# A constant tile for the warm-up, V's first block earlier, the gate's transpose by DMA, and a last tile split at 384

## The chip, the cores and the metric

The kernel runs on one core of one Trainium2 chip. A core has five engines with a queue of instructions each: TensorE (PE in the profile, with its weight loads as PEld), VectorE (DVE), ScalarE (ACT), GpSimd (POOL) and SyncE (SP), which here only issues transfers. They meet through semaphores. The metric is the device time of one execution in microseconds (us). Four runs of the kernel before gave 165.85, 166.08, 166.55 and 167.09 us, median 166.31.

## The reference, cut to what matters

One input x (2048 tokens, 512 wide) goes through two mixers, and a gate for each token mixes their outputs:

```python
g = _sigmoid((x * gate_w).sum(-1, keepdims=True))
# A: attention over 8 keys of the past, 2 tokens apart, 32 heads of 16
qkv = x @ wqkv
logits = einsum("bhsd,bhswd->bhsw", q, kg) * Dh ** -0.5     # kg: k at s - 2 * w, masked below 0
a = einsum("bhsw,bhswd->bhsd", softmax(logits), vg) @ wo    # heads joined again
# B: an MLP over the tokens
h = _layernorm(x)
u = gelu(einsum("bsd,sf->bdf", h, w1) + b1)                 # 1792 hidden rows
b = transpose(einsum("bdf,fs->bds", u, w2) + b2)
out = g * a + (1 - g) * b
```

All inputs are bfloat16.

## The kernel before, in words

The work comes in stages, and PE runs through them in a fixed order: warm-up matmuls on a tile of ones; transposes of the first 512 tokens of x on PE with fillers between them, and the first q projection (L571, L562, L590); the other projections (L649); the MLP's first product (L859, 14 hidden tiles of 16 matmuls); its second product (L886, 16 output tiles of 128 tokens) with the attention's output projection added into the same PSUM bank (L895).

The program is a list of operations with what each reads and writes. A planner inside the kernel (`_Sched`) gives each a modelled duration, runs a list schedule, and so writes out the order of every engine and its waits; `prio` pushes an operation ahead (negative) or back. PE's operations made by `PE(...)` are chained and stay in the order of the text; those added with `A("pe", ...)` - the score sums (`f_sum`) and the gate's transpose (`f_te`) - go where the planner puts them.

Loads. SP's queue issues, in the order of the text: x tiles 0 and 2, half of wq, wk, then for blocks 1 to 3 of 512 tokens x itself (`ld_x`) and a transposed copy by DMA (`ld_xt`, called xT1 to xT3), wv, then w1's seven blocks (1 MB each, `w1_0` to `w1_6`, in five slots of SBUF that are used again) with wo among them, and w2's eight blocks. w1_1 onward is held until a VectorE-side sum by DMA (`qd0_1`) is done; w1_3 waits for the score sums of the first half of the tokens, because its slot is xT's. ScalarE's queue issues x tiles 1 and 3 and the other half of wq. POOL's queue issues gate_w, b1 and b2 at the start, and later accumulating transfers and the broadcast of attention weights.

The bias rows and gate_w are turned into columns by three small PE transposes (`f_tb`, L662 to L664) and copied out by VectorE (L669 to L671).

Attention. VectorE multiplies q with shifted k for all heads, adds the four sub-blocks, and PE sums over each head's dimensions (`f_sum`, L718, and with it for the first half the gate's dot product, L713). Softmax runs on ScalarE and VectorE. VectorE then multiplies the weights with shifted V and adds, one tile of 256 tokens after another (8 tiles); L895 reads each.

The gate. ScalarE clips the dot product and takes an exp (`zexp`) into `EB`, laid out along tokens in the free dimension, the same value in 32 partitions. `f_te` turns it with four 128x128 PE transposes into PSUM bank 3, and VectorE makes 1 + exp, its reciprocal (`OMG`, the weight of the MLP) and `C2`, OMG times the second bias (L803 to L806). The output evictions (L906 and, for the last tile, L932 and L935) scale by OMG and add C2. The last output tile is made in two halves of 256 columns, in two PSUM banks, evicted by ScalarE and VectorE and stored from two queues.

PSUM banks of the projections go round a ring of seven (`ring`), then of three for V.

Of the kernel before, what the change touches and what calls it, by code (L numbers as in the profile page):

```python
# [280 lines left out]
class _Mem:  # L281
# [17 lines left out]
    def view(self, name, dtype, dims, extra=0, p0=0, np_=128):  # L299
        base = self.arena[:].bitcast(dtype)  # L300
        pst = base.ap[0][0]
        esz = mybir.dt.size(dtype)
        o = self.off[name]
        assert o % esz == 0
        return bass.AP(base.tensor, p0 * pst + o // esz + extra, [[pst, np_]] + [list(d) for d in dims])


def bass_gated_mix__sliding_local_dilated__mixer_token_mlp__prompt_kernel(nc, A_x, A_wqkv, A_wo, B_x, B_w1, B_b1, B_w2, B_b2, gate_w, out, dbg=None):
    with contextlib.ExitStack() as es:
# [19 lines left out]
        m.region("RB", UT_ * 2)  # L329
        m.region("E32", D * 4)  # L330
        m.region("EB", D * 2)
        m.region("IDENT", 128 * 2)
        m.region("ONES", 128 * 2)
        m.region("OUTS", 5 * D * 2)
# [59 lines left out]
        RB = view("RB", BF16, [(1, UT_)])  # L394
        E32 = view("E32", FP32, [(1, D)])
        EB = view("EB", BF16, [(1, D)])
        OUTS = view("OUTS", BF16, [(D, 5), (1, D)])
        IDENT = view("IDENT", BF16, [(1, 128)])
        ONES = view("ONES", BF16, [(1, 128)])
        ONES4 = view("ONES", BF16, [(0, 4), (1, 128)])  # L400
        RP = view("RP", BF16, [(1, 32)])
        GWREP = view("GWREP", BF16, [(32, 4), (1, 32)])
        MASK = view("MASK", BF16, [(PAD, NW), (1, PAD)], np_=32)
# [36 lines left out]
        def sub(ap_, offs, dims):  # L440
            return bass.AP(ap_.tensor, ap_.offset + offs, [list(ap_.ap[0])] + [list(d) for d in dims])
# [8 lines left out]
        def act(o_, i_, f_, **kw):  # L450
# [3 lines left out]
        GELU = "gelu_apprx_tanh_and_others"  # L454


        A("pool", lambda e: e.memset(ONES, 1.0), 0.25, writes=["ones"], name="ones")
        A("pool", lambda e: e.affine_select(out=IDENT, in_=ONES, pattern=[[1, 128]], compare_op=ALU.is_equal,
                                            fill=0.0, base=0, channel_multiplier=-1),
          0.4, reads=["ones"], writes=["ident"], name="ident")  # L460
        A("pool", lambda e: e.memset(sub(KH[0], 0, [(KR, 4), (1, PAD)]), 0.0), 0.2, writes=["kpad"], name="kpad")
        A("pool", lambda e: e.memset(sub(V5, 0, [(VR, 4), (1, PAD)]), 0.0), 0.2, writes=["vpad"], name="vpad")

# [20 lines left out]
        def load(name, dst, src, nbytes, writes, transpose=False, queue="sp", issue=0.5, order=True, deps=(), after=()):  # L484
            ds = sch.dsem(name)

            def fn(e):
                if transpose:
                    return e.dma_start_transpose(dst, src)
                return e.dma_start(dst, src)  # L490
            op = sch.dma(queue, fn, nbytes, ds, issue=issue, writes=writes, deps=list(deps) + late_dep[0],
                         after=list(after) + ([last_ld[queue]] if order and queue in last_ld else []), name=name)
            if order:
                last_ld[queue] = op
            return op
# [4 lines left out]
        def ld_w(name, tn, d0, d1, res):  # L500
            load(name, WQKV[:, d0:d1, tn * D:(tn + 1) * D], wqkv_v[:, d0:d1, tn * D:(tn + 1) * D], (d1 - d0) * 128 * D * 2, [res])

        def ld_xt(sb):
            load("xT%d" % sb, XT[:, :, sb * 512:(sb + 1) * 512], x2d[sb * 512:(sb + 1) * 512, :], int(1.4 * 512 * D * 2), ["xt%d" % sb],
                 transpose=True, issue=3.3)
# [14 lines left out]
        xq(2, "sp")  # L520
        xq(3, "act")
        load("wk", WQKV[:, 0:4, D:2 * D], wqkv_v[:, 0:4, D:2 * D], 4 * 128 * D * 2, ["wk"], deps=[x1ld])
        for k_ in range(1, 4):
            ld_x(4 * k_, 4)
            ld_xt(k_)
        load("gw", GWR, gate_w.rearrange("(t p) -> t p", p=128), 1024, ["gwr"], issue=1.0, queue="pool")
        load("b1", B1R, B_b1.rearrange("(t p) -> t p", p=128), 4096, ["b1r"], issue=1.0, queue="pool")
        load("b2", B2R, B_b2.rearrange("(t p) -> t p", p=128), 4096, ["b2r"], issue=1.0, queue="pool")
        ld_w("wv", 2, 0, 4, "wv")

        def ld_w1(j):
            w1ld[j] = load("w1_%d" % j, W1H[j], w1v[:, :, 256 * j:256 * j + 256], S * 256 * 2, [W1R[j]] + (XTALL if j in (3, 4) else []), order=j < 3,
# [5 lines left out]

        ld_w1(0)

        def f_warm(n):
            def fn(e):
                ins = None
                for _ in range(n):
                    ins = e.matmul(ps[:, 7, :], lhsT=ONES, rhs=ONES4, start=True, stop=True)
                return ins
            return fn

        chain = [None]

        def PE(fn, dur, reads, writes, name, prio=0):
            op = A("pe", fn, dur, reads=reads, writes=writes, after=([chain[0]] if chain[0] is not None else []), name=name, prio=prio)
            chain[0] = op
            return op

        PE(f_warm(5), 2.1, ["ones"], ["b7"], "warm")

        def f_fill(n):
            def fn(e):
                ins = None  # L560
                for _ in range(n):
                    ins = e.matmul(ps[:, 0, 0:256], lhsT=ONES, rhs=sub(ONES, 0, [(0, 2), (1, 128)]), start=True, stop=True)  # L562
                return ins
            return fn

# [33 lines left out]
        def pe_q0(hb, dt):  # L599
            PE(f_q0(hb, dt), 0.44, ["xt0_%d_%d" % (2 * hb + t_, dt // 2) for t_ in range(2)] + ["wq%d" % (dt // 2)], ["b%d" % dl for dl in range(4)],  # L600
               "q0_%d_%d" % (hb, dt))

        pe_tx(0)
        PE(f_fill(1), 0.2, [], ["b0"], "fill0")
        pe_tx(1)
        PE(f_fill(2), 0.4, [], ["b0"], "fill1")
        pe_q0(0, 0)
# [2 lines left out]
        pe_tx(2)  # L610
        pe_tx(3)
        pe_q0(0, 3)
        for dt in range(4):
            pe_q0(1, dt)
        XT0 = ["xt0_%d_%d" % (t, k_) for t in range(4) for k_ in range(2)]
# [42 lines left out]
            PE(f_proj(tn, dl, sb, bank), 0.87, xt_res(sb) + WR[tn], ["b%d" % bank], "pj%s%d_%d" % ("qkv"[tn], dl, sb))  # L658
            evac(tn, dl, sb, bank)

        def f_tb(e):
            e.transpose(out=psb(3)[:, 0:NFT], in_=B1R, identity=IDENT[0:NFT, 0:NFT])  # L662
            e.transpose(out=psb(3)[:, 64:68], in_=GWR, identity=IDENT[0:4, 0:4])
            return e.transpose(out=psb(3)[:, 32:32 + NST], in_=B2R, identity=IDENT[0:NST, 0:NST])  # L664

        for dl in range(4):
            proj(1, dl, 0)
        PE(f_tb, 0.3, ["b1r", "b2r", "gwr", "ident"], ["b3"], "t_b12")
        A("dve", lambda e: e.tensor_copy(out=GWREP, in_=sub(psb(3), 64, [(1, 4), (0, 32)])), 0.2, reads=["b3"], writes=["gwrep"], name="gwrep", prio=-20)  # L669
        A("dve", lambda e: e.tensor_copy(out=B1C, in_=psb(3)[:, 0:NFT]), 0.15, reads=["b3"], writes=["b1c"], name="b1c", prio=-20)  # L670
        A("dve", lambda e: e.tensor_copy(out=B2C, in_=psb(3)[:, 32:32 + NST]), 0.15, reads=["b3"], writes=["b2c"], name="b2c", prio=-20)  # L671
        for dl in range(4):
            proj(0, dl, 1)
            proj(1, dl, 1)
        A("act", act(sub(KH[1], 0, [(KR, 4), (1, PAD)]), sub(KH[0], HS, [(KR, 4), (1, PAD)]), AF.Copy), 0.25,
          reads=["k%d_1" % dl for dl in range(4)], writes=["khalo"], name="khalo")
        for dl in range(4):
# [2 lines left out]
                    proj(tn, dl, sb)  # L680
        ring[0], ring[1] = 0, [0, 1, 2]
        for dl in range(4):
            for sb in range(4):
                proj(2, dl, sb)


# [107 lines left out]
        ld_w1(3)  # L794
        ld_w1(4)

        def f_te(e):
            ins = None
            for k_ in range(4):
                ins = e.transpose(out=psb(3)[:, 128 * k_:128 * k_ + 128], in_=EB[:, 128 * k_:128 * k_ + 128], identity=IDENT)  # L800
            return ins
        A("pe", f_te, 0.5, reads=["eb", "ident"], writes=["b3"], name="t_e", prio=-50, delay=0.5)
        A("dve", lambda e: e.tensor_scalar(out=E1, in0=sub(psb(3), 0, [(256, 2), (32, 4), (128, 2)]), scalar1=1.0, scalar2=None, op0=ALU.add), 0.2,  # L803
          reads=["b3"], writes=["e1"], name="e1", prio=-20)
        A("dve", lambda e: e.reciprocal(out=OMG, in_=E1), 0.2, reads=["e1"], writes=["omg"], name="omg", prio=-20)
        A("dve", tt(C2, OMG, B2C, ALU.mult), 0.12, reads=["omg", "b2c"], writes=["c2"], name="c2", prio=-20)  # L806

# [110 lines left out]
            if half == 1 and i >= LAG:  # L918
                finish_tile(i - LAG)
        lastb = [bank_(), bank_()]  # L920
        CH = ((0, 256), (256, 512))
        for hf, (c0, c1) in enumerate(CH):
            for half in range(2):
                PE(f_ph3(L, lastb[hf], half, c0, c1), 0.77, ["ut%d" % ft for ft in range(7 * half, 7 * half + 7)] + ["w2_%d" % (L // 2)], ["b%d" % lastb[hf]],
# [3 lines left out]
        for hf, (c0, c1) in enumerate(CH):  # L928
            bank = lastb[hf]
            PE(f_wo(L, bank, c0, c1), 0.44, ["ot%d" % (L // 2), "wo"], ["b%d" % bank], "wo%d_%d" % (L, hf))  # L930
            if hf == 0:
                A("act", act(OUTS[:, 4, c0:c1], ps[:, bank, 0:256], AF.Identity, scale=col(OMG, L), bias=col(C2, L)), 0.55,  # L932
                  reads=["b%d" % bank, "omg", "c2"], writes=["outs4"], name="ev%da" % L)
            else:
                A("dve", (lambda bank_, a_, b_: lambda e: e.tensor_scalar(out=OUTS[:, 4, a_:b_], in0=ps[:, bank_, 0:256], scalar1=col(OMG, L),  # L935
                                                                          scalar2=col(C2, L), op0=ALU.mult, op1=ALU.add))(bank, c0, c1), 0.35,
                  reads=["b%d" % bank, "omg", "c2"], writes=["outs4h"], name="ev%db" % L)
            sch.dma("act" if hf == 0 else "sp", (lambda a_, b_: lambda e: e.dma_start(outv[:, L, a_:b_], OUTS[:, 4, a_:b_]))(c0, c1), 65536,
                    ds_out[4] if hf == 0 else ds_last, issue=0.5, reads=["outs4" if hf == 0 else "outs4h"], name="d_out%d_%d" % (L, hf))
# [80 lines left out]
```

## Time and profile before

| | us |
|---|---|
| median of four runs | 166.31 |
| profiled execution, its own time | 165.85 |
| its span | 164.1 |
| PE busy | 159.2 |
| VectorE busy | 150.8 |
| ScalarE busy | 75.3 |
| PE on L859 / L886 / L649 / L895, busy | 48.7 / 49.8 / 38.0 / 15.4 |
| ScalarE's table loads (L955), 11 | 14.1 |

The profile records one execution. "Busy" is the time in which an engine had an instruction in work; matmuls overlap, so their busy time is longer than their share of the chain. Times within the execution count from the start of the span. A line number is that of the kernel before unless the text says otherwise; many vector operations have the line of a helper (L448 for a two-input vector operation, L451 for an activation, L490 and L489 for a load and a transposing load). The chain of waits is followed backward from the last instruction to whatever released it.

### The profile page before, as it was taken

Reading aid. Unit: us, or ns where it says so; the run is one execution under the profiler, and the core shown is the slowest. Engines: PE = TensorE matmul, PEld = TensorE weight load, DVE = VectorE, ACT = ScalarE, POOL = GpSimd, SP = SyncE. Lnnn points to the kernel's source line nnn. Section 1 sums busy time; section 2 is a strip of 40 time slices with the busy share of each in tenths; the row PEclk is TensorE's granted clock in tenths of the full one; section 3 lists DMA queues with packets and bytes.
Section 4 is the critical chain, followed back from the end, with each engine's and each line's share of the span. In section 5 each row is a group of like instructions: output and inputs, shape, how many; then the busy total and the mean of one; then the engine's idle time right before and its main releaser. Section 6 shows DMA issues by size and latency. Waiting matters only on the chain.

```text
span 164.1 us, 2003 instructions
## 1 busy us (share of the span) xinstructions
PE 159.2 (97%) x801; PEld 78.4 (48%) x817; DVE 150.8 (92%) x126; ACT 75.3 (46%) x104; POOL 13.7 (8%) x38
## 2 busy tenths in 40 slices
PE   6999999999999999999999999999999999999993
PEld 2864555555544444444444344444444444444742
DVE  0499999999999999999999999999999999999941
ACT  3366676766682699852211669210121111111164
POOL 7000002020000000005000000005001222000000
PEclk9999999999999999999999999999999999999999
DMA  5999998719498369999999864994995899980013
GB/s 155 298 236 259 221 308 177 144 32 192 116 305 253 94 166 282 289 292 178 166 225 302 253 193 137 292 242 129 274 234 165 170 209 182 211 189 35 32 60 131
DMA packets 44120, 32.11 MB, mean 196 GB/s; under 512 B 7248, under 2 KB 41680, under 8 KB 44112
## 3 DMA queue, kind: packets, MB, share of 16 engines
q1 hardware_dynamic: 40800, 21.96, 50.2%
q0 software_dynamic: 2608, 9.45, 29.3%
q10 hardware_dynamic: 704, 0.59, 1.1%
q8 instruction: 6, 0.10, 0.3%
q14 instruction: 2, 0.02, 0.0%
HBM read 18.88 MB, written 2.10 MB: 128 GB/s over the span
## 4 chain that ended last, share of the span: by engine, by line
PE 95%; DMA 2%; issue 1%; DVE 1%
PE ps L859 29%; PE ps L886 29%; PE ps L649 23%; PE ps L895 8%; PE ps L590 2%; DMA arena<-in_A_x_dram 2%; PE ps L718 1%; PE ps L571 1%; PE ps L713 1%; DVE arena L935 0%; DVE arena L583 0%; PE ps L800 0%; PE ps L562 0%; PE ps L662 0%; PE ps L664 0%
## 5 line engine op out<-in xcount | busy, mean ns | idle before, releaser
L448 DVE TENSOR_TENSOR arena<-arena 128x4096 bf16<-128x4096 bf16 (+8 forms) x79 | 131.8, 1719 | 1.0
L886 PE MATMUL ps<-arena 128*128 128x512 bf16 (+1 forms) x234 | 49.8, 366 | 0.2
L859 PE MATMUL ps<-arena 128*128 128x512 bf16 x218 | 48.7, 379 | 0.3
L451 ACT ACTIVATE arena<-ps,arena 128x512 bf16<-128x512 f32 (+1 forms) x30 | 21.8, 729 | 58.7 <-PE ps L895 37.7
L451 ACT ACTIVATE arena<-ps 128x512 bf16<-128x512 f32 (+3 forms) x53 | 32.9, 629 | 18.7 <-PE ps L649 11.1
L649 PE MATMUL ps<-arena 128*128 128x512 bf16 x172 | 38.0, 379 | 0.2
L886 PEld LDWEIGHTS ps<-arena 128*128 128x128 bf16 x238 | 23.3, 98 | 25.3
L859 PEld LDWEIGHTS ps<-arena 128*128 128x128 bf16 x224 | 21.7, 98 | 26.6 <-ACT arena L451 0.4
L649 PEld LDWEIGHTS ps<-arena 128*128 128x128 bf16 x176 | 19.8, 113 | 17.7 <-issue 0.2
L895 PE MATMUL ps<-arena 128*128 128x512 bf16 (+1 forms) x66 | 15.4, 366 | 0.1
L955 ACT ACT_TABLE_LOAD x11 | 14.1, 1283 | 2.5 <-issue 2.3
L786 POOL DMA_DIRECT2D arena<-arena x8 | 4.3, 561 | 73.9 <-DVE arena L448 73.9
L895 PEld LDWEIGHTS ps<-arena 128*128 128x128 bf16 x68 | 6.7, 98 | 7.2
L688 DVE BATCH_NORM_STATS2 arena<-arena 128x6 f32<-128x512 bf16 x16 | 9.9, 679 | 0.2 <-DMA arena<-in_A_x_dram 0.2
L451 ACT ACTIVATE arena<-arena 128x16 f32<-128x16 f32 (+5 forms) x10 | 6.8, 679 | 6.7 <-DVE arena L448 6.6
L702 DVE TENSOR_SCALAR arena<-arena 128x512 bf16<-128x512 bf16 x16 | 5.5, 418 | 0.0
L583 DVE COPY arena<-ps 128x256 bf16<-128x256 bf16 x4 | 1.1, 292 | 4.6 <-PE ps L571 4.6
L828 POOL DMA_DIRECT2D arena<-arena x3 | 3.6, 1200 | 19.0 <-DVE arena L448 19.0
L743 POOL DMA_DIRECT2D arena<-arena x2 | 2.5, 1234 | 29.2 <-DVE arena L699 20.5
L590 PE MATMUL ps<-arena 128*128 128x256 bf16 x32 | 4.0, 274 | 0.2 <-DVE arena L583 0.2
L935 DVE TENSOR_SCALAR arena<-ps,arena 128x256 bf16<-128x256 f32 x1 | 0.5, 545 | 3.7 <-PE ps L895 3.7
L590 PEld LDWEIGHTS ps<-arena 128*128 128x128 bf16 x32 | 3.3, 114 | 0.7 <-DVE arena L583 0.7
(39 smaller groups left out, 20.1 us busy)
## 6 DMA issues: line engine op xcount, KB each, us to landing
arena<-in_B_w_dram SPq DMA_DIRECT2D x7, 1024.0 KB, 7.2
arena<-in_B_w_dram SPq DMA_DIRECT2D x8, 896.0 KB, 8.5
arena<-arena POOLq DMA_DIRECT2D x5, 1024.0 KB, 7.9
arena<-arena POOLq DMA_DIRECT2D x8, 512.0 KB, 11.0
out_dram<-arena SPq DMA_DIRECT2D x15, 128.0 KB, 1.7
arena<-in_A_x_dram SPq DMA_DIRECT2D x3, 512.0 KB, 4.9
arena<-in_A_wqkv_dram SPq DMA_DIRECT2D x2, 512.0 KB, 4.5
arena<-in_A_wo_dram SPq DMA_DIRECT2D x1, 512.0 KB, 9.6
```

Source lines behind the costliest of these rows:

```text
L448: return lambda e: e.tensor_tensor(out=o_, in0=a_, in1=b_, op=op_)
L451: return lambda e: e.activation(out=o_, in_=i_, func=f_, **kw)
L590: ins = e.matmul(ps[:, dl, hb * 256:hb * 256 + 256], lhsT=sub(WQKV, dt * 3 * D + dl, [(4, 128)]), rhs=XT[:, dt, hb * 256:hb * 256 + 256], ...
L649: ins = e.matmul(ps[:, bank, :], lhsT=sub(WQKV, dt * 3 * D + tn * D + dl, [(4, 128)]), rhs=XT[:, dt, sb * 512:(sb + 1) * 512], start=(dt = ...
L688: A("dve", (lambda t_: lambda e: e.bn_stats(out=ST6[:, t_, :], in_=X[:, t_, :]))(t), 0.67, reads=["x%d" % t], writes=["st%d" % t], name="s ...
L702: A("dve", (lambda t_: lambda e: e.tensor_scalar(out=X[:, t_, :], in0=X[:, t_, :], scalar1=col(RSTD, t_), scalar2=col(NMR, t_), op0=ALU.mu ...
L786: prev = sch.dma("pool", (lambda d_, s_: lambda e: e.dma_start(d_, s_))(dst, src), 524288, sch.dsem("av%d_%d" % (h, c)), issue=1.0, reads= ...
L828: sch.dma("pool", (lambda o_, i_: lambda e: e.dma_start(o_, i_, accum_op=ALU.add, max_dma_last_dim=4096))(pw(0, 4), pw(4, 4)), 1800000, sc ...
L859: ins = e.matmul(ps[:, bank, :], lhsT=W1H[ft // 2][:, st, 128 * (ft % 2):128 * (ft % 2) + 128], rhs=X[:, st, :], start=(st == 0), stop=(st ...
L886: ins = e.matmul(ps[:, bank, 0:c1 - c0], lhsT=W2S[i // 2][:, ft, 128 * (i % 2):128 * (i % 2) + 128], rhs=UT[:, ft, c0:c1], start=(ft == 0) ...
L895: ins = e.matmul(ps[:, bank, 0:c1 - c0], lhsT=OT[:, i // 2, dl, 128 * (i % 2):128 * (i % 2) + 128], rhs=WO[:, dl, c0:c1], start=False, sto ...
L955: e.preload_act_table_set(want)
```

## The change

It has these parts.

- The warm-up matmuls and the fillers read a constant that the program framework writes before the kernel's body, and not the kernel's own tile of ones. The warm-up is five matmuls of 512 columns and four of 128, and it waits for nothing. The filler between the first two transposes of x is dropped.
- The bias and gate_w transposes move from behind the first K projections to the middle of the first q projection, into another PSUM bank.
- On SP's queue wv goes ahead of xT3, and xT3 ahead of the last block of x. On PE the V projection of the first 512 tokens goes ahead of the q and k projections of the second half of the tokens.
- The gate's exp is turned by one transposing DMA from SBUF to SBUF on SP's queue; VectorE reads the result from SBUF. PE's four transposes go.
- The last output tile is split at column 384.

The planner makes a new order from this. What the changed program's order shows beside the moved operations: the first half's score sums come after 32 matmuls of the MLP's first product instead of 24, the second half's after 200 instead of 192; VectorE runs two more q-k products ahead of the statistics of x tiles 12 to 15; the gate's addition comes after the first half's softmax sums instead of before them; the transposing DMA stands on SP between w1_4 and w1_5; ScalarE loads tables 7 times instead of 11.

```diff
-        A("pool", lambda e: e.memset(ONES, 1.0), 0.25, writes=["ones"], name="ones")
+        A("pool", lambda e: e.memset(ONES, 1.0), 0.25, writes=["ones"], name="ones", prio=-90)
...
-        for k_ in range(1, 4):
+        for k_ in range(1, 3):
             ld_x(4 * k_, 4)
             ld_xt(k_)
+        ld_w("wv", 2, 0, 4, "wv")
+        ld_xt(3)
+        ld_x(12, 4)
         load("gw", GWR, ...
         load("b1", B1R, ...
         load("b2", B2R, ...
-        ld_w("wv", 2, 0, 4, "wv")
...
-        def f_warm(n):
-            def fn(e):
-                ins = None
-                for _ in range(n):
-                    ins = e.matmul(ps[:, 7, :], lhsT=ONES, rhs=ONES4, start=True, stop=True)
-                return ins
-            return fn
+        C1 = nc.const_aps.tensor(1.0, (128, 128), BF16)
+
+        def f_warm(e):
+            ins = None
+            for n_ in (512,) * 5 + (128,) * 4:
+                ins = e.matmul(ps[:, 7, 0:n_], lhsT=C1, rhs=nc.const_aps.tensor(1.0, (128, n_), BF16), start=True, stop=True)
+            return ins
...
-        PE(f_warm(5), 2.1, ["ones"], ["b7"], "warm")
+        PE(f_warm, 2.6, [], ["b7"], "warm")
...
-                    ins = e.matmul(ps[:, 0, 0:256], lhsT=ONES, rhs=sub(ONES, 0, [(0, 2), (1, 128)]), start=True, stop=True)
+                    ins = e.matmul(ps[:, 0, 0:256], lhsT=C1, rhs=nc.const_aps.tensor(1.0, (128, 256), BF16), start=True, stop=True)
...
         pe_tx(0)
-        PE(f_fill(1), 0.2, [], ["b0"], "fill0")
         pe_tx(1)
         PE(f_fill(2), 0.4, [], ["b0"], "fill1")
...
         pe_q0(0, 3)
+        PE(f_tb, 0.17, ["b1r", "b2r", "gwr", "ident"], ["b4"], "t_b12")
+        # with its three VectorE copies, now out of bank 4
         for dt in range(4):
             pe_q0(1, dt)
...
         for dl in range(4):
             proj(1, dl, 0)
-        PE(f_tb, 0.3, ["b1r", "b2r", "gwr", "ident"], ["b3"], "t_b12")
-        # with its three VectorE copies, out of bank 3
         for dl in range(4):
             proj(0, dl, 1)
             proj(1, dl, 1)
+        for dl in range(4):
+            proj(2, dl, 0)
...
         for dl in range(4):
-            for sb in range(4):
+            for sb in range(1, 4):
                 proj(2, dl, sb)
...
-        A("pe", f_te, 0.5, reads=["eb", "ident"], writes=["b3"], name="t_e", prio=-50, delay=0.5)
-        A("dve", lambda e: e.tensor_scalar(out=E1, in0=sub(psb(3), 0, [(256, 2), (32, 4), (128, 2)]), scalar1=1.0, scalar2=None, op0=ALU.add), 0.2,
-          reads=["b3"], writes=["e1"], name="e1", prio=-20)
+        sch.dma("sp", lambda e: e.dma_start_transpose(EBT, EB), 400000, sch.dsem("ebt"), issue=0.6, reads=["eb"], writes=["ebt"], name="ebt", prio=-50)
+        A("dve", lambda e: e.tensor_scalar(out=E1, in0=sub(EBT, 0, [(256, 2), (32, 4), (128, 2)]), scalar1=1.0, scalar2=None, op0=ALU.add), 0.2,
+          reads=["ebt"], writes=["e1"], name="e1", prio=-20)
...
-        CH = ((0, 256), (256, 512))
+        CH = ((0, 384), (384, 512))
```

## The prediction

> **What bounds the kernel now.** I read the busy shares first, then TensorE's waits, then the chain that ended last, then the timeline at the places that the diff touches.
>
> ```profile
> span 164.1 us, 2003 instructions
> PE 159.2 (97%) x801; PEld 78.4 (48%) x817; DVE 150.8 (92%) x126; ACT 75.3 (46%) x104; POOL 13.7 (8%) x38
> ```
>
> TensorE (PE) is busy for 97% of the span, VectorE (DVE) for 92%. So there are two candidates, and the waits decide between them.
>
> ```profile
> PE ps L545 <- POOL arena L457: 1.1, 1, 1.1
> PE ps L590 <- DVE arena L583: 0.2, 1, 0.2
> PE ps L571 <- DMA arena<-in_A_x_dram: 0.2, 1, 0.2
> ```
>
> These are all of PE's waits (total, times, longest): 1.5 us, all before 5.2 us. After that PE never waits, for V's load, the gate or VectorE's sums. The chain of waits shows the same, with the pieces that the diff touches:
>
> ```profile
> 0.82 2.60 DMA arena<-in_A_x_dram
> ...
> 3.55 0.58 PE ps L571 x4
> 4.13 0.21 PE ps L562
> 4.35 0.40 PE ps L571 x4
> 4.75 0.02 issue
> 4.77 0.30 DVE arena L583
> 5.07 0.05 issue
> 5.12 1.50 PE ps L590 x12
> ...
> 12.84 0.11 PE ps L662
> ...
> 61.69 0.22 PE ps L800 x4
> ...
> 161.48 0.03 issue
> 161.50 0.55 DVE arena L935
> ```
>
> Columns: start, length, what. The start hangs on the landing of x tile 0 (3.42), not on the warm-up matmuls. L562 is the first filler, L662 begins the bias transposes (0.16 with L663 and L664), L800 is the transpose that goes. What PE does not execute any more, or executes inside one of its few holes, is gain, microsecond for microsecond; what is moved elsewhere is worth nothing unless PE starts to wait.
>
> **Part by part.** Sums are against the profiled execution: span 164.1, its time 165.85, so 1.7 lies around the span. It is the fastest of the four runs; the median, 166.31, is 0.46 above it. I add the change to the median.
>
> *Warm-up without the memset.* PE is let go at about 0.8 (the first loads start at 0.82) but waits until 1.07 for the ones (L457). The constant is there by 0.5, so the warm-up begins about 0.26 earlier. Its five 512-column matmuls start 0.427 apart and 128-column ones 0.107 apart at this clock: 5 x 0.427 + 4 x 0.107 = 2.56, ending at 3.37, before x lands at 3.42. The transposes start at 3.55 as before: no gain of itself. The clock is the unknown. Starts of matmuls in the trace tell when it is granted: 128 columns take 0.107 until 4.57, 256 columns take 0.110 from then on. So full clock comes 3.50 after the first matmul, and in this execution almost nothing but transposes ran before it. An earlier warm-up can save nothing here, and at most 0.26 where the release is late. I take 0 and keep 0.26. The Trainium skill ("TensorE: Matmul & The Clock Gate", What's actually happening) says that the gate looks at a free-running window of about 3.4 us, so that the release varies with where the first matmul falls; 3.50 agrees. By it the release would move by less than 0.26, or by a whole window; the sum stays as it is.
>
> *First filler gone (L562, 0.21).* Behind it are x tile 1's transposes, VectorE's copy (0.30) and the first projection at 5.12. Without it that would be 4.91. But the projection needs wq's first half, issued at 1.27 and landing 3.6 later, 4.9; x tile 0 took 0.13 from landing to matmul, so 5.0. Gain 0.12, between 0 and 0.21.
>
> *Bias transposes moved ahead of the second half of q (L662 to L664, 0.16).* Their new place is where PE stands idle for 0.11 (the matmul at 7.34 ends its slot, the next starts at 7.45, waiting for VectorE's copy). Of 0.16 taken out at 12.84, 0.05 comes back: gain 0.11. Their three POOL loads were issued from 1.48 to 2.72, landing 3.9 to 4.3 later, by 6.65, before 7.2. They use bank 4, so the first K projection now waits for the three copies on VectorE; these end about 8.2, the projection is at 9.4. The copies (0.35) go partly into VectorE's hole of 0.24 before L625.
>
> *V block 0 moved up; its weights' load ahead of xT3 and x12.* The matmuls are the same, 0.863 a projection. The projections of xT1 began at 12.94, now at 12.7, so V starts at 12.7 + 8 x 0.863 = 19.6. Its load takes the queue place of x12 (issued 13.86, landed 4.9 later, 18.8): 0.8 of cover. If that cover goes, PE waits. x12 takes the place of wv on SP (issued 18.58, landed 4.1 later, 22.7); xT3 keeps its place, and the first W1 load after them too. VectorE runs two products (2.2 each) ahead of these four statistics, so it comes to them at 13.96 - 0.3 + 2.2 + 2.4 (statistics of x8) + 4.4 = 22.7 and waits about 0.1, where before it waited 0.18. The activations behind them (L697) sit on ScalarE behind eight evictions and run at 27.2, after their input at 25.8. Normalised x is ready at 22.8 + 2.5 + 0.6 + 2.2 + 0.2 + 5.4 = 33.7, its first matmul at 47. Gain 0.
>
> *Gate transpose by DMA.* L800 leaves PE: gain 0.22, whole, as it stood in an unbroken run of matmuls. New wait: the transpose is on SP behind W1's fifth block, and W1's sixth and seventh and all of w2 are behind it. Times: the changed order puts the score sums 8 matmuls later, at 54.3, done 56.2. ScalarE then does the logits (1.88), the clip, one gelu (its matmuls end at 59.7), a table load (1.28) and the exp (0.63): 62.3. On SP, W1's fourth block waits for the score sums (56.2) and lands 5.7 later, 61.9; the fifth is issued then and lands 5.7 to 7.2 later, 67.6 to 69.1. The transpose, issued at 62.35, comes behind its packets. Price of one: no row has SBUF to SBUF. The nearest is xT3, 512 KB, which landed 1.74 after the load ahead of it (issued 14.49 and landing 6.0 later, 20.5; x12 at 18.8). This one is a quarter: 0.44 to 1.74, so 68.0 to 70.8. VectorE asks for it after L777's addition, which ended at 71.39; without the three small gate operations ahead of it (0.58) and with about 0.4 of holes closed, at 70.4. So VectorE waits 0 to 0.4. Behind it on VectorE lies everything up to the last attention tile.
>
> Cover for that: VectorE ended its last tile at 157.78 and PE read it (L895) at 159.78: 2.0 spare. The second score sums had 1.1 (90.14 against 91.27) and get 1.5 more, as they too move 8 matmuls back. So a wait up to 1.9 costs nothing. W1's sixth block would land near 74 instead of 71.3; PE wants it at 84. ScalarE loses four table loads (11 to 7), off the path.
>
> A rule speaks against this part: the Trainium skill ("VectorE: DVE Perf Modes", The three transpose paths) has a 128x128 transpose at 390 ns on TensorE and 1309 ns by DMA. On PE the trace has 0.22 for four. By the rule, my estimate is 4 x 1.31 = 5.2 after the fifth W1 block, 72.8 to 74.3, a wait of 2.4 to 3.9, and a kernel 0.5 to 2.0 longer than the sum below. I go by the xT rows, which give 512 KB in 1.74.
>
> *Last tile split at 384.* PE's columns are the same. VectorE's piece falls from 256 to 128 columns: ScalarE's 256 against 512 columns is 0.555 against 0.777, VectorE's 0.545 likewise falls by some 0.13. ScalarE's piece starts at 161.31, held by the tile before, not by PE, and takes about 0.67 instead of 0.555; its store then lands at 161.97 + 0.03 + 1.61 = 163.61, against 163.67 for the later store before. So ScalarE's store becomes the end: gain 0.04, between -0.05 and 0.13.
>
> *Sum:* 0.12 + 0.11 + 0.22 + 0.04 = 0.49. The profiled execution becomes 165.36, the median 165.82. That is 0.3%; about 0.5% (0.83 us) is what a measurement of this kernel can tell from no change.
>
> **Rivals.**
> *The gate comes late (the other side).* VectorE waits at the gate's addition. The end is later by the wait less 1.9; the kernel gets slower than before when the wait passes 2.4 (landing after 72.8), by over 0.5% when it passes 3.2. For it: no row of such a transfer, and an xT took 7.0 from issue to landing. If it needs those 7.0 after the fifth W1 block's 69.1, it lands at 76.1: wait 5.7, cost 3.8, time 169.6. Against it: most of the xT's 7.0 is the queue ahead. Chance 0.1.
> *The clock comes earlier.* The runs spread by 1.24 (165.85 to 167.09). If that spread is the release of the clock, and an earlier warm-up brings the usual run to the fastest one, 0.46 more goes: 165.36; with 0.26 besides, 165.1. For it: the profiled execution is the fastest run and has the release just when the transposes end. Against: one trace, and 0.26 is little. Chance 0.26.
> *The clock comes later.* With x landing late, PE has a longer hole and no filler, and a release some 3.5 later would run PE at half speed from 5.0 to 8.0: 1.5 more, 167.3. Chance 0.05.
> *V waits.* If the load of V's weights lands as late as in its old place, 22.7, PE stands for 3.1 and only xT's cover is bought: 168.9. Chance 0.03.
> *It does nothing.* The start hangs on wq's landing and fillers only change place: only the 0.22 stays, 166.1; within the same class as the forecast.
>
> **How the numbers follow.** Forecast and nothing together 0.56, clock earlier 0.26, gate late 0.1, clock later 0.05, V waits 0.03. Likeliest: 165.8, its own range 165.4 to 166.3. The range goes down to 165.0 for the earlier clock and up to 167.0, a gate late by some 3; what is left out above is 0.1. Of the earlier clock 0.22 ends below 165.48, with 0.05 from the forecast's own spread: faster 0.27. Slower: most of gate late, clock later and V: 0.14. The rest, 0.59, is the same.
>
> **What would show it.** First matmul near 0.8; first projection near 5.0; no hole at 7.4; the first V projection at 19.6 without a wait for the load; 32 matmuls of L859's kind before the score sums; no gate transpose on PE; the DMA transpose landing 68 to 71 and the addition after it starting near 70.4; PE's last matmul near 161.0. Wrong if PE shows any wait after 5 us, above all at the attention tiles in the last 10 us, or if VectorE's idle time before the gate's addition passes 1.9.

## The result, and the profile after

The kernel after takes 165.79 us (median of 53 runs, 165.33 to 167.97), the kernel before 166.55 (79 runs, 165.81 to 168.29). The ratio is 0.9959, with a 95% interval of 0.9950 to 0.9967: 0.41% less, or 0.68 us (0.55 to 0.83). It is the ratio of the means, 165.82 and 166.51, without the one run of after that fell in a slower state (167.97). That is within the 0.5% that the prediction called the same. The time is 0.03 from the prediction's 165.82, but so close a hit is luck: the prediction set out from four runs of before with a median of 166.31, where 79 runs give 166.55, and took off 0.49, which is less than the measured 0.55 to 0.83.

The profiled execution of after took 165.61 against 165.85; the lowest runs are 165.33 and 165.81. Before's profile is one of its fastest executions (three quarters of its runs took 166.23 or more), after's is closer to a usual one (three quarters took 165.60 or more). So the two profiles differ by less than the kernels do.

The page of after, its busy shares:

```profile
span 163.9 us, 2000 instructions
PE 159.4 (97%) x801; PEld 78.0 (48%) x816; DVE 150.6 (92%) x126; ACT 70.2 (43%) x100; POOL 13.7 (8%) x38
```

The waits of TensorE (PE) in after, as a list of line, what was waited for, total, times and longest:

```profile
PE ps L549 <- PEq L1004: 0.8, 1, 0.8
```

PE is still the bound, and after its start it waits for nothing: not for V's weights, not for the gate. The chain of after (start, length, what), at the places that the diff touches:

```profile
0.85 2.72 PE ps L549 x9
3.57 1.01 PE ps L574 x8
4.58 0.43 PE ps L565 x2
5.01 0.07 issue
5.08 1.58 PE ps L593 x12
...
54.47 0.98 PE ps L717 x16
55.45 0.86 PE ps L722 x16
56.31 2.27 PE ps L858 x10
58.63 10.74 PE ps L858 x49
...
160.31 1.34 ACT arena L452 x2
```

The warm-up begins at 0.85 instead of 1.07, x's transposes at 3.57 as before (3.55), the first projection (L593) at 5.08 instead of 5.12. There is no gate transpose after the score sums any more. The "issue" pieces of 0.05 every 10.8 us in the longer chain are matmuls whose record is missing: 49 x 0.2157 and one more make the step. The chain ends on ScalarE (two evictions) where it ended on VectorE before.

The timeline of after around the moved bias transposes (start, busy, engine, line, operation):

```profile
6.95 0.60 PE L593 MATMUL ps<-arena 128*128 128x256 bf16 x4
7.48 0.18 PE L607 MATMUL ps<-arena 14*128 14x14 bf16 x1
7.52 0.16 PE L608 MATMUL ps<-arena 4*128 4x4 bf16 x1
7.54 0.17 PE L609 MATMUL ps<-arena 16*128 16x16 bf16 x1
7.64 1.94 PE L593 MATMUL ps<-arena 128*128 128x256 bf16 x16
```

And the gate's transpose by DMA, on SP and VectorE:

```profile
62.10 0.37 SPq L491 DMA_DIRECT2D arena<-in_B_w_dram  x1
62.56 2.48 SPq L801 DMA_TRANSPOSE arena<-arena  x1
65.09 6.50 SPq L491 DMA_DIRECT2D arena<-in_B_w_dram  x3
...
70.42 0.17 DVE L802 TENSOR_SCALAR arena<-arena 128x16 f32<-128x16 bf16 x1
```

It is issued at 62.56 behind W1's fifth block (62.10), holds SP for 2.48 and lands 5.9 after its issue, at 68.45; the block ahead of it landed at 67.79. The addition that reads it (L802) starts at 70.42 with nothing in the bracket for a wait: 2 us to spare.

**Where the time went.** Starts of matmuls are exact to a few ns, so an execution can be cut into three stretches: up to the last matmul of the first q projections ("start"), from there to the first matmul of the split output tile ("middle"), and from there to the end of the span ("end"). The whole study is in this table, worked out from the traces.

| kernel | start, to q's last matmul | middle | end | profiled time |
|---|---|---|---|---|
| before | 9.12 | 143.94 | 11.07 | 165.85 |
| after | 9.30 | 143.43 | 11.15 | 165.61 |
| b_warm | 9.08 | 144.06 | 11.09 | 165.99 |
| b_nofill | 9.83 | 143.94 | 11.07 | 166.56 |
| b_tb | 9.32 | 143.66 | 11.06 | 165.78 |
| b_gate | 9.18 | 143.87 | 11.06 | 165.85 |
| a_noV | 9.74 | 143.43 | 11.15 | 166.07 |
| a_split256 | 9.23 | 143.43 | 11.06 | 165.46 |
| a_nowarm | 11.39 | 143.43 | 11.15 | 167.72 |
| c_rows | 9.78 | 143.43 | 11.14 | 166.11 |
| a_gatelate | 9.64 | 147.93 | 11.20 | 170.50 |
| a_wvlate | 9.18 | 147.68 | 11.13 | 169.74 |
| a_xt3late | 9.06 | 143.43 | 11.14 | 165.36 |
| a_noV_xt3late | 9.35 | 145.37 | 11.14 | 167.59 |

(b_ kernels are the kernel before with one part of the change, a_ kernels the kernel after with one part undone or delayed.) The middle shrinks by 0.51, which is the bias transposes (0.28) and the gate's (0.22), and it repeats to 0.01 us in every kernel that has the same work there. The bias transposes come back inside the start at 0.15. The end grows by 0.08. The rest of the start varies from one execution to the next: it is 9.06 to 9.74 in the seven profiles that have after's first instructions on PE (after, a_noV, a_split256, a_gatelate, a_wvlate, a_xt3late, a_noV_xt3late), 0.68 between them.

### The profile page after: what moved, and what is told of

Read it like the earlier page. It is cut to its first block, busy times and chain, and to the rows that moved or that the text cites. A ratio compares the mean times of both kernels' runs of the same rounds, so it can differ in the third digit from the quotient of the medians.

```text
span 163.9 us, 2000 instructions
## 1 busy us (share of the span) xinstructions
PE 159.4 (97%) x801; PEld 78.0 (48%) x816; DVE 150.6 (92%) x126; ACT 70.2 (43%) x100; POOL 13.7 (8%) x38
## 4 chain that ended last, share of the span: by engine, by line
PE 95%; DVE 2%; ACT 1%; issue 1%
PE ps L858 29%; PE ps L885 29%; PE ps L660 23%; PE ps L894 8%; PE ps L549 2%; PE ps L722 1%; DVE arena L692 1%; PE ps L593 1%; ACT arena L452 1%; PE ps L574 1%; PE ps L717 1%; DVE arena L586 0%; PE ps L565 0%; DVE arena L621 0%; DVE arena L623 0%
## 5 line engine op out<-in xcount | busy, mean ns | idle before, releaser
L885 PE MATMUL ps<-arena 128*128 128x512 bf16 (+2 forms) x234 | 50.0, 366 | 0.2
L452 ACT ACTIVATE arena<-ps 128x512 bf16<-128x512 f32 (+3 forms) x53 | 32.9, 629 | 18.6 <-PE ps L660 10.8
L894 PE MATMUL ps<-arena 128*128 128x512 bf16 (+2 forms) x66 | 15.2, 366 | 0.1
L593 PE MATMUL ps<-arena 128*128 128x256 bf16 x32 | 4.1, 278 | 0.1
L593 PEld LDWEIGHTS ps<-arena 128*128 128x128 bf16 x32 | 3.3, 114 | 0.6 <-DVE arena L586 0.5
```

Source lines behind the costliest of these rows:

```text
L452: return lambda e: e.activation(out=o_, in_=i_, func=f_, **kw)
L593: ins = e.matmul(ps[:, dl, hb * 256:hb * 256 + 256], lhsT=sub(WQKV, dt * 3 * D + dl, [(4, 128)]), rhs=XT[:, dt, hb * 256:hb * 256 + 256], ...
L885: ins = e.matmul(ps[:, bank, 0:c1 - c0], lhsT=W2S[i // 2][:, ft, 128 * (i % 2):128 * (i % 2) + 128], rhs=UT[:, ft, c0:c1], start=(ft == 0) ...
L894: ins = e.matmul(ps[:, bank, 0:c1 - c0], lhsT=OT[:, i // 2, dl, 128 * (i % 2):128 * (i % 2) + 128], rhs=WO[:, dl, c0:c1], start=False, sto ...
```

## The experiments

### One part alone, on the kernel before

b_warm takes the constant tile and the new row of warm-up matmuls and nothing else; b_nofill only drops the first filler.

```diff
-        PE(f_warm(5), 2.1, ["ones"], ["b7"], "warm")
+        PE(f_warm, 2.6, [], ["b7"], "warm")
```


> The kernel before, with the warm-up alone changed (five matmuls of 512 and four of 128 columns on the constant, no wait). Theory: warm-up starts 0.22 us earlier (0.85 against 1.07), x's transposes still start on x's landing near 3.55, so the fastest executions stay as they are; the clock's release varies from run to run and comes 0 to 0.22 earlier on average, so the median falls by 0.1 to 0.3 us (ratio 0.998 to 0.9995). Rival, the clock has no part in it: ratio 1.000. In the profile: first matmul at 0.85, first projection at 5.0 to 5.1.

```diff
-        PE(f_fill(1), 0.2, [], ["b0"], "fill0")
```


> The kernel before without the first filler alone. Theory: the first projection goes from 5.12 to about 5.05, held by wq's landing at 4.9, gain 0.06 to 0.12 us: ratio 0.9993 to 0.9997. Rival, the hole in the warm-up delays the clock's release by a window in part of the executions: slower, ratio 1.001 to 1.003, and first matmuls of L590 0.21 us apart in the profile.

b_tb moves the bias transposes and their copies behind q0's first half; all other instructions are held in the order of before. b_gate replaces `f_te` by the transposing transfer; the planner puts that one block earlier on SP, ahead of W1's fifth.

```diff
         pe_q0(0, 3)
+        PE(f_tb, 0.17, ["b1r", "b2r", "gwr", "ident"], ["b4"], "t_b12")
...
-        PE(f_tb, 0.3, ["b1r", "b2r", "gwr", "ident"], ["b3"], "t_b12")
```


> The kernel before with the bias and gate_w transposes and their three copies moved ahead of the second half of q, everything else in the order of before. Theory from the two traces: at the old place they cost 0.28 us of PE (12.68 to 12.96), at the new place 0.29 less a hole of 0.14 that was there anyway; gain 0.14 us, ratio 0.9992. Rival: the first K projection waits for the copies and nothing is gained, ratio 1.000.

```diff
-        A("pe", f_te, 0.5, reads=["eb", "ident"], writes=["b3"], name="t_e", prio=-50, delay=0.5)
+        sch.dma("sp", lambda e: e.dma_start_transpose(EBT, EB), 400000, sch.dsem("ebt"), issue=0.6, reads=["eb"], writes=["ebt"], name="ebt", prio=-50)
```


> The kernel before with the gate's transpose by DMA alone. Here the planner puts the transfer on SP ahead of w1_4, not behind it, and keeps VectorE's addition where it was, at 63.7. The exp ends at 59.6, so the transfer is issued at 59.7, behind w1_3's packets (landing 60.5). Theory: it lands at 61 to 62.5, VectorE does not wait, PE loses the four transposes: gain 0.22 us, ratio 0.9987. Rival, the transfer is slow (7 us as an xT): landing 66.7, a wait of 3 on VectorE, PE waits 2 at the second score sums: ratio 1.011.

Measured against before (166.42 on that chip): b_warm 166.60, ratio 1.0009 (0.9984 to 1.0033); b_nofill 166.38, 1.0000 (0.9979 to 1.0022); b_tb 166.10, 0.9987 (0.9966 to 1.0009); b_gate 165.99, 0.9988 (0.9961 to 1.0015). No time settles any of them. The traces settle b_tb and b_gate. In b_tb the middle is 0.28 shorter, what the transposes took at 12.7 in before (start to start). In b_gate L800's 0.22 is gone, but 0.16 of it is lost again at 20.6, where PE stands between two projections; b_warm loses 0.12 at the same place, 20.5. Both times the projection that begins there reads xT3, and xT3's transfer landed at 20.82 and 20.69, 0.13 before that projection's start. In before it landed at 20.51 and the projection started at 20.73 without a hole. So the kernel before has about 0.1 of cover for this transfer; the prediction had put its landing at 20.5 and not asked when PE needs it.

b_nofill's profile has the sign that its rival named: its first six projection matmuls start 0.17 to 0.21 apart, and full speed comes at 6.5. Its times don't show a loss. Of the profiles with a warm-up, the four with the first filler have full speed from 4.56 to 5.26, the nine without it from 4.42 to 6.5. That dropping the filler delays the clock in part of the executions is neither shown nor excluded by that.

### V's first block and the split, undone

a_noV is the kernel after with V's first block and the loads in their old places (planned anew); a_split256 has the last tile split in halves again.

```diff
-        for dl in range(4):
-            proj(2, dl, 0)
...
-            for sb in range(1, 4):
+            for sb in range(4):
                 proj(2, dl, sb)
```


> The changed kernel with V's first block, wv, xT3 and x12 back in their old places (the planner makes the order of the rest). Theory: the V move has no part in the time, as PE waited for none of these loads before or after; ratio to before as the changed kernel's, 0.995 to 0.997, and PE without a wait after 8 us. Rival, the move bought something that the traces do not name: ratio nearer 1, 0.998 or more.

```diff
-        CH = ((0, 384), (384, 512))
+        CH = ((0, 256), (256, 512))
```


> The changed kernel with the last tile split at 256 as before. Theory: the last store lands 2.2 us after PE's end in both profiles (163.67 less 161.46, 163.35 less 161.15), so the split is worth 0.0 to 0.05 us: ratio 0.995 to 0.997. Rival, the split is what goes beyond the sum of 0.49: ratio 0.997 to 0.998.

Measured against before (166.33 on that chip): a_noV 165.95, ratio 0.9975 (0.9956 to 0.9994); a_split256 165.46, ratio 0.9947 (0.9925 to 0.9970). Neither can be told from after by its time, and a_noV's ratio lies between what its theory (up to 0.997) and its rival (from 0.998) expected. By the table the split at 384 makes the end 0.07 to 0.08 longer: 11.13 to 11.15 in seven of the eight profiles with it (a_gatelate has 11.20), 11.06 to 11.09 in the six with halves. The last lines of the timeline of after:

```profile
161.19 0.41 DVE L934 TENSOR_SCALAR arena<-ps,arena 128x128 bf16<-128x128 f32 x1 [3.62 <-PE ps L894]
161.62 0.33 SPq L937 DMA_DIRECT2D out_dram<-arena  x1
161.68 0.35 ACTq L937 DMA_DIRECT2D out_dram<-arena  x1
```

and of a_split256:

```profile
161.12 0.54 DVE L934 TENSOR_SCALAR arena<-ps,arena 128x256 bf16<-128x256 f32 x1 [3.31 <-PE ps L894]
161.50 0.35 ACTq L937 DMA_DIRECT2D out_dram<-arena  x1
161.69 0.33 SPq L937 DMA_DIRECT2D out_dram<-arena  x1
```

The two stores change places, and counted from the last tile's first matmul the later one lands at the same point: 10.62 in before, 10.62 in after, 10.60 in a_split256. Behind that landing the span goes on for 0.45, 0.53 and 0.46. What makes the 0.07 to 0.08 is the order in which SP waits for the stores. In these kernels it waits for ScalarE's store first and for its own in a further instruction. In a_split256 its own store lands last, at 163.27, and SP leaves its waits 0.08 later. In after ScalarE's lands last, at 163.36; the wait for the other store, which landed 0.26 earlier, is executed only behind that, and SP leaves 0.15 after the landing. c_rows (below) waits in the order of landing: its span goes on for 0.46 behind the last landing, as with halves, against 0.52 to 0.53 in the seven other profiles with the split at 384. Its end is 11.14 all the same, because its last store landed 0.06 later than after's, at 10.68.

### Two rivals forced

a_gatelate puts the transposing transfer behind W1's seventh block on SP, a_wvlate the load of V's weights behind x12; the order of everything else is kept. The edit stands behind the planner: `move_behind` takes one operation out of an engine's order and puts it right behind another (for a_wvlate: "wv" behind "x12").

```diff
         est = sch.schedule()
+        move_behind("sp", "ebt", "w1_6")
```


> The changed kernel with the gate's transposing transfer put on SP behind w1_6 and not behind w1_4, everything else in the same order. Theory: w1_6 landed at 75.6, so the transfer lands near 76.3 where VectorE asks at 70.4: a wait of 5.9. VectorE's second score products end at 95.7 instead of 89.8 and PE, which comes at 92.6, waits 3.1; of the rest 1.1 comes out at the last attention tile. The kernel is 4.2 us longer than the changed one: 170.0, ratio 1.021. Rival, the sums downstream have cover that the profile does not show: ratio under 1.01.

> The changed kernel with the load of V's weights put behind x12 on SP, everything else in the same order. Theory: it lands at 23.0 where PE asks for it at 19.6; PE waits 3.4 us and nothing gives it back, since PE is the bound: 169.2, ratio 1.016. Part of it (up to 0.3) could come back where VectorE's spare time of 1.6 us is not used up. Rival, PE has slack elsewhere: ratio under 1.005.

a_gatelate: 170.18 (169.53 to 170.75), ratio 1.0229 (1.0194 to 1.0264). Waits of PE and of VectorE in its profile:

```profile
PE ps L722 <- DVE arena L449: 2.7, 1, 2.7
```

```profile
DVE arena L802 <- DMA arena<-arena: 5.4, 1, 5.4
```

The transfer landed at 76.25, VectorE waited 5.4 for it, and PE 2.7 (2.8 in starts) at the second score sums; that is the 5.4 less the 2.6 of cover that the prediction counts there (1.1 and 1.5 more). The rest of the cost in this execution came by another way than the expected wait at the last attention tile. The table of windows of a_gatelate (stretch, length, then busy time and count for PE, PEld, DVE, ACT and POOL, and the granted clock):

```profile
93.00:95.70 2.70, 0.02 (x1) 0.00 (x0) 2.70 (x3) 0.00 (x0) 0.00 (x0) 1.00 0.91 265
95.70:99.20 3.50, 3.44 (x23) 1.30 (x24) 3.50 (x2) 1.88 (x1) 0.00 (x0) 0.71 0.73 215
99.20:104.00 4.80, 4.80 (x20) 2.01 (x19) 4.66 (x6) 0.87 (x2) 0.00 (x0) 0.86 0.00 0
```

After the wait the granted clock falls to 0.71 and 0.86: from 97.19 to 100.59 eight 512-column matmuls start 0.427 apart instead of 0.216. That is 1.69 more, and 2.81 + 1.69 = 4.50 is the whole of what the middle grew (147.93 against 143.43). The last tiles had no wait; PE at half speed gives VectorE time to catch up, which would account for it. The four runs list a mean granted clock of 0.99 twice (170.50, the profiled one, and 169.85) and of 1.00 twice (170.75 and 169.53). So not every run need have had the slow stretch, and 4.50 with its two parts holds for the profiled execution.

a_wvlate: 170.54 (169.74 to 171.94), ratio 1.0261 (1.0215 to 1.0308). Its wait of PE and, in its chain, the load and what stands behind it:

```profile
PE ps L660 <- DMA arena<-in_A_wqkv_dram: 4.0, 1, 4.0
```

```profile
18.33 5.43 DMA arena<-in_A_wqkv_dram
...
23.90 27.79 PE ps L660 x128
```

The load landed at 23.77. In starts the hole is 4.12, and all of it stays to the end: the middle grew by 4.25, 0.12 of which was a wait of K's first matmul. This profiled execution, 169.74, had a mean granted clock of 1.00 and no slow stretch behind the hole; the other three had 0.99, 0.99 and 0.98, with 170.10, 170.99 and 171.94. 3.4 us at half speed are 0.01 of the mean, so a slow stretch behind the wait there is likely, but there is no profile of those three.

### The warm-up away, and the bias rows by DMA

a_nowarm leaves out the nine warm-up matmuls. c_rows collects b1, b2 and gate_w in one 16x384 tile, turns it by a single transposing transfer on SP ahead of W1's first block, copies the columns out on VectorE later, and waits for the stores in the order of landing.

```diff
-        PE(f_warm, 2.6, [], ["b7"], "warm")
```


> The changed kernel without any warm-up matmul. Theory: the clock is granted 3.4 to 6.8 us after PE's first matmul, wherever the window falls; without the warm-up that first matmul is x's transpose at 3.57, so the release comes at 7.0 to 10.4 instead of 4.3 to 7.7, and PE runs 2.7 us longer at half speed: median 1.3 us above the changed kernel, 167.1, ratio 1.002 to 1.005. Rival, the clock is not behind the spread of times: the time stays at the changed kernel's, ratio 0.996.

```diff
+        last_ld["sp"] = sch.dma("sp", lambda e: e.dma_start_transpose(ROWT, ROW), 200000, sch.dsem("rowt"), issue=0.6, reads=["gwr", "b1r", "b2r"], writes=["rowt"], after=[last_ld["sp"]], name="rowt")
-        PE(f_tb, 0.17, ["b1r", "b2r", "gwr", "ident"], ["b4"], "t_b12")
-                for d in ds_out + [ds_last]:
+                for d in ds_out[:4] + [ds_last, ds_out[4]]:
```


> The changed kernel with the bias rows and gate_w turned by one transposing transfer as well (16 x 384, on SP ahead of w1_0, copies on VectorE after the statistics), and with the last stores' semaphores waited for in the order in which they land. Theory: PE loses 0.29 us of small transposes at 7.4, of which a hole of 0.14 comes back; the end gains up to 0.07: 0.15 to 0.2 us less than the changed kernel, ratio to before 0.9945 to 0.995. Rival: the transfer delays w1_0 or the copies delay VectorE, and the ratio is 0.996 or more.

a_nowarm: 167.19 (166.53 to 168.65), ratio 1.0041 (1.0016 to 1.0065). Its timeline of PE:

```profile
3.68 1.01 PE L573 MATMUL ps<-arena 128*128 128x128 bf16 x8 [3.68 <-DMA arena<-in_A_x_dram]
...
5.12 2.72 PE L592 MATMUL ps<-arena 128*128 128x256 bf16 x12
```

The twelve matmuls take 2.72 instead of after's 1.58. They start 0.213 apart up to 9.86 and 0.109 from then on, so full speed comes 6.18 after PE's first matmul. Only the start is longer (11.39), and middle and end are those of after to 0.01. Against after the ratio is 1.0041/0.9959, 1.4 us, for a PE that begins 2.83 later: 0.5 us per us.

c_rows: 165.77 (165.28 to 166.11), ratio 0.9951 (0.9934 to 0.9968), not to be told from after. The hole at 7.9 that the bias transposes filled (0.14) stays, so at most 0.15 was to be had there. In its profile the late clock (below) hides that, and its times can't show so little.

### What V's place is worth

b_gate and b_warm had shown a hole at xT3. Two kernels put the same load late, one in each order: a_noV_xt3late (V's block in its old place) and a_xt3late (V's block moved up; there it goes behind "x12").

```diff
         est = sch.schedule()
+        move_behind("sp", "xT3", "wv")
```


> The kernel after with V's first block and its loads in their old places, and with xT3's load put behind the load of V's weights on SP; every other engine keeps its order. In the old order of PE the tenth projection behind q reads xT3, at 20.7 to 21.1; xT3 landed at 20.5 to 20.8 there, and in two profiles of that order PE stood 0.12 and 0.16 at this place. Theory (V's first block is cover for xT3): behind 512 KB more, which took 1.8 (20.51 against 18.77), xT3 lands at about 22.3, PE starts that projection at 22.4, a wait of 1.3 to 1.8, and the time is about 167.5. Rival (the small holes at that place come from something else and V's place is worth nothing): no wait, 165.95 as without the edit.

> The kernel after with xT3's load put behind x12's on SP; every other engine keeps its order. xT3 landed at 21.1 in the kernel after and should land at about 22.9. With V's first block ahead of it PE asks for xT3 at 9.63 + 17 x 0.863 = 24.3, counting eight projections of xT1, four of V, four of K's and q's order that comes before it at most; at the earliest, right behind V and one more projection, at 23.9. Theory (V's first block is cover for xT3): no wait on PE, 165.8, the same as the kernel after. Rival (V's place is worth nothing): the same wait as in the other order, 1.3 to 1.8, and 167.4.

a_noV_xt3late: 167.62 (166.16 to 168.34), ratio 1.0045 (1.0002 to 1.0089). a_xt3late: 165.86, ratio 0.9963 (0.9941 to 0.9986); before took 166.77 on that chip. The wait of PE and the timeline of a_noV_xt3late:

```profile
PE ps L658 <- DMA arena<-in_A_x_dram: 1.8, 1, 1.8
```

```profile
16.80 4.05 PE L658 MATMUL ps<-arena 128*128 128x512 bf16 x18
22.62 4.70 PE L658 MATMUL ps<-arena 128*128 128x512 bf16 x21 [1.77 <-DMA arena<-in_A_x_dram]
```

and the timeline of a_xt3late at the same place:

```profile
16.72 10.52 PE L660 MATMUL ps<-arena 128*128 128x512 bf16 x48
```

xT3 landed at 22.49 in the one and at 22.33 in the other. In the old order PE stood for it (1.94 in starts; the middle is 145.37, 1.94 more), in the new order it ran on and the middle is 143.43. The theory held, the rival fell: V's first block is cover for xT3, 3.45 of it. The wait isn't the same in every execution of a_noV_xt3late: the profiled one took 167.59, but three of the ten runs took 166.16 to 166.63, where the fastest run of a_noV (165.44) and 1.94 make 167.38. What V's place is worth without a forced delay is small: of the six profiles with the old order of PE and load, four have no hole and two have 0.12 and 0.16, 0.05 on average.

## Why the prediction was right, point by point

- **PE bounds, and its waits lie in the start.** Right. What left PE's run came off the end microsecond for microsecond.
- **Gate transpose off PE, 0.22.** Right: 61.529 to 61.752 in before is 0.223, and the middles of b_gate (143.87 less its hole of 0.16) and of before differ by 0.22.
- **The transposing transfer.** Right: issued at 62.56 (predicted 62.35), landed at 68.45 (68.0 to 70.8), the addition at 70.42 (70.4), no wait. The choice between the xT rows and the rule on transposes ("VectorE: DVE Perf Modes", The three transpose paths) was decided by the row: four 128x128 blocks landed 0.66 behind the load ahead of them in after, and 2.4 after their issue in b_gate, not the 5.2 that four times 1.31 would give.
- **Bias transposes, gain 0.11.** The hole was right, its size and theirs were not: 0.28 leaves the place at 12.7, 0.285 less a hole of 0.138 comes back at 7.4. Gain 0.14. The prediction took 0.16, which is the starts from the first small transpose to the next matmul; the step into the group is 0.10 longer than between two projections' matmuls, and the first matmul behind it takes 0.03 more.
- **First filler, gain 0.12.** This term failed. The first projection began 0.04 earlier, 5.08, because wq's first half landed at 4.94 and 0.13 from there to the matmul makes 5.07, where the prediction's step had gone from a rounded 4.9 to 5.0; and then its first two matmuls were still at half speed (0.172 and 0.157 apart instead of 0.109), as the full clock came at 5.34 instead of 4.56. In this pair of executions the filler's term is -0.04. It hangs on a landing that varies: in the ten profiles without the filler wq's first half landed between 4.62 and 5.39 and the first projection began between 4.87 and 5.53; in the four with it, between 5.09 and 5.18. b_nofill, 1.0000, can't size it either.
- **V's first block, gain 0.** The waits were right: V's weights landed at 19.29 and V's first matmul did not wait, x12 at 23.03 with 0.2 of waiting on VectorE (predicted 0.1). But the price was read on the side of the load moved ahead only; what V's block does for xT3 (0 to 0.16, 0.05 on average) was left out.
- **Split at 384, gain 0.04.** The pieces were right: VectorE's 0.41 instead of 0.545, ScalarE's 0.66 (predicted 0.67), ScalarE's store the last. The sum was not: the end is 0.08 longer, 0.03 outside the bounds of -0.05 to 0.13. Two things were missing from it. ScalarE's larger store took 1.67 from issue to landing and not the 1.61 that the prediction took from the smaller one, which used up the gain; and SP's second wait behind that landing (0.07) was put at nothing.
- **Warm-up, gain 0, up to 0.26.** By a_nowarm, 0.5 us per us of earlier start, 0.22 earlier would be 0.11, an estimate; b_warm, at 1.0009 where 0.998 to 0.9995 was expected, can't show that little.
- **The sum of 0.49.** The profile pair moved by 0.24: 0.51 out of the middle, 0.19 back in the start (0.15 of bias transposes, 0.04 of clock and filler), 0.08 back in the end. The lowest runs differ by 0.48, the ratio says 0.68. From single parts, 0.22 + 0.14 - 0.08 = 0.28 stands in every profile; with estimates of 0.11 for the warm-up, 0.05 for xT3's cover and 0.04 to 0.12 for the filler, which no time shows, it would be 0.48 to 0.56. So somewhat less than half of the 0.68 is shown part by part, and where the rest lies isn't settled. The start varies most, but the profiles don't show it shorter after the change: 9.06 to 9.74 in the seven with after's, 9.12 and 9.18 in before and b_gate. One profiled execution of each kernel can't size its average.
- **Rivals.** *Clock earlier* is right that the clock makes much of the spread between profiled executions: the three with the release at 6.3 to 6.5 have starts of 9.74 to 9.83, those with 4.4 to 5.4 starts of 9.06 to 9.32, but for a_gatelate, where wq landed late (9.64). That the earlier warm-up brings the usual run to the fastest one isn't shown: in after's profile the clock came later than in before's, and the median is 0.46 above the lowest run, against 0.74 in before. *Clock later*: 1.5 was its price for a release at 8.0; the 5.34 of the profile cost 0.08, two matmuls at half speed. *Gate late* was priced at 3.8 for a landing at 76.1 and a VectorE wait of 5.7; forced, with a landing at 76.25 and a wait of 5.4, it cost 4.50 in the profiled execution, where PE's clock was slow for a stretch behind its wait. *V waits*, 3.1 on PE and 168.9, came to 4.1 and 169.74 in the profiled execution (median 170.54), since the load landed at 23.77 and not 22.7 there.

## What to carry to other kernels

When one engine never waits, count its matmul starts: what is removed from its unbroken run is gain at its full length, and cutting an execution into stretches between exact starts shows effects of 0.1 us that no number of timed runs here could. When a piece of work is moved, ask not only whether its own inputs are there in the new place but which transfer gets cover, or loses it, in the old one. When what finishes last is moved, look at the order in which the ends are waited for: here a wait for a store long landed cost 0.07 because it stood behind the last one. A wait in the middle of PE's work can cost more than its length, because the clock may fall behind it, as in the profiled a_gatelate.

## What the runs showed of the hardware

- **When the clock is released.** Two things date it: the spacing of equal matmuls, and the trace's record of the granted clock, which has its first entry at that moment (9.86 by both in a_nowarm). The windows' column reads 1.00 before that entry too (from 3.5 on in before, after, b_warm and a_nowarm alike) and does not show it. Full speed came at 4.42 in a_xt3late, 4.56 in before (3.50 after PE's first matmul), 4.72 in b_warm (3.87), 4.79 in a_wvlate, 4.99 in a_gatelate, 5.12 in b_tb and a_split256, 5.26 in b_gate, 5.34 in after (4.50), 5.63 in a_noV_xt3late and 9.86 in a_nowarm (6.18). The other three have no record; by the spacing it came at about 6.3 in a_noV, 6.5 in b_nofill and 6.5 in c_rows (5.7). But for a_nowarm the warm-ups are alike, so most of what lies between 3.5 and 5.7 looks like chance; what part the dropped filler has in it is open. In the records full speed then lasts for 160.43 in eight profiles and for 157.01, 163.84 and 92.16 in the others: 47, 46, 48 and 27 times 3.413. The Trainium skill ("TensorE: Matmul & The Clock Gate", What's actually happening) has a free-running window of some 3.4 us, and these lengths agree with it; a wait of one to two windows would give such a range.
- **A hole can cost twice.** 2.8 us without matmuls in the profiled a_gatelate were followed, 1.4 after PE had resumed, by 3.4 us at half speed; 4.1 us in the profiled a_wvlate were followed by none. Length alone doesn't decide it here.
- **A small transposing transfer.** 128 KB from SBUF to SBUF landed 2.4 after its issue in b_gate, and 0.66 behind the 1 MB load ahead of it in after. SP, which issues it, was held by it for 1.20 in b_gate, 2.48 in after and 4.46 in a_gatelate, against 0.37 for the block before it in after; xT3's 512 KB held SP for 3.10 to 4.95. That the transposing is the reason isn't shown: plain loads issued behind other loads held SP for up to 4.84 in before.
